# Causal convolution and top-2 mixture of experts: memory of their own for block rows, and the second and third unit's convolution shared anew

## The chip, the cores and the metric

One core of one Trainium2 chip. The metric is the device time of one execution in microseconds, before against after; the time before is the median of three runs. A profile is one further execution, seen by the hardware profiler.

Engines: TensorE (PE; PEld is its weight load), VectorE (DVE), ScalarE (ACT), GpSimd (POOL) and SyncE (SP), which here only issues DMAs. A name with a q behind it (SPq) is an engine's queue of issues.

## The reference

```python
def _attn_ref(x, weight):                    # x (8, 3584, 192), weight (8 heads, 7 taps)
    w = softmax(weight, axis=-1)
    x_pad = np.concatenate([np.zeros((B, 6, D)), x], axis=1)
    x_unf = x_pad[:, idx, :].reshape(B, S, K, H, group)       # 7 rows up to the token's own
    return np.einsum('hk,bskhg->bshg', w, x_unf).reshape(B, S, D)

def _moe_ref(x, w_gate, w_noise, noise, w1, w2):   # 28672 tokens, 8 experts, 192 -> 1024 -> 192
    noisy_logits = x @ w_gate + np.log1p(np.exp(x @ w_noise)) * noise
    top2 = ...                               # the two largest, softmax of the two: top2_w
    for e in range(E):
        for k in range(2):
            mask = top2[:, k] == e
            h = np.maximum(x[mask] @ w1[e], 0.0)
            out[mask] += top2_w[mask, k, None] * (h @ w2[e])
```

## The kernel before

The 28672 tokens are worked on in 28 units of 1024 tokens (128 partitions with 8 tokens each). A unit is convolved (`conv`, or on TensorE by `conv_pe` with a diagonal 128 x 128 matrix for each head and tap), scaled by a power of two and split into a high and a low float16 part (`rb`), gated (`gating`: transposes, 40 small matmuls, log1p, the top two, the rank in each expert's list), and then each token's row is scattered twice to a region in DRAM, `xs`, by 16 indirect DMAs of GpSimd. Rounds of blocks read these regions: in round j each expert takes one block (128 rows in round 0, 256 after). A block loads its rows transposed (`load_block`, tile `bT`), multiplies them with `w1` in two halves of 512 hidden columns (`mm1`, five float16 matmuls for each 128 columns), takes the Relu on ScalarE and its low part on VectorE (`h`), multiplies with `w2` (`mm2`), scales by the gate on ScalarE and adds to the output by an indirect DMA of GpSimd. `load_meta` loads the token numbers and gates of a round's rows, once for all experts. Blocks are loaded two ahead.

The weights are prepared in place, part by part (`prepare`): a part (e, c) is scaled on ScalarE into a float16 high part, and the low part is the difference, taken on VectorE or, for nine parts in `POOL_LO`, on GpSimd; then ScalarE writes the scaled original too. A part's high and low half lie where the part before it lay as loaded, so the next part's ScalarE step waits for the low part of the one before. Parts 0 and 1 of an expert are `w1`, 2 and 3 are `w2`. Gram products on TensorE give the scales, for two experts at a time; `allsum` is a small matmul that adds over partitions.

The order on TensorE, VectorE, ScalarE and SyncE is that of the program; GpSimd's is found by the scheduler. The program's order is written out by hand for the first three units, in `ORDER`. Each letter is one step of a generator in `streams`: `a`, `b`, `e`, `E` a head on TensorE for units 0, 1, 2, 2; `c`, `d`, `f` the rest of the convolution of units 0, 1, 2 (maximum, scale, split); `g`, `h`, `i` the gating of units 0, 1, 2; `w` a step of the preparation; `v`, `V` evacuations of unit 2's heads from PSUM; `1`, `2` the six rows that a unit takes over from the unit before (`halo`); `D` diagonals; `l`, `x` loads. The text up to the first bar runs before the blocks; each part between bars is the side work of one slot, and a block has two slots, one behind each half of `mm1`. When the parts are used up, `Side.slot` fills the slots by itself, by a credit in microseconds (`FREE`) against each step's planned cost, the number that it yields.

Memory: the diagonals are in a pool `start` that is closed when the written order is over; the pool `ffn` (`bT`, `mt`, `h`, `y`) is opened in the memory that becomes free. PSUM has two buffers `ph` and two `py`; unit 1 and the second half of unit 2 use `ph`, the first half of unit 2 `py`.

Of the kernel before, what the change touches and what calls it, by code (L numbers as in the profile page):

```python
# [19 lines left out]
P = 128  # L20
# [5 lines left out]

ORDER = "Daaaacwccc1xcnwcwcgnwglgggbbwbwggwgwbbwwwbbbww2eeeedddwdwddvhEEwhEEhhh|hw|hw|hww|ww|ww|Vfw|fw|fw|fww|fww|fww|iww|iww|ii|i|i|i|i"

# [4 lines left out]
def kernel(  # L33
# [44 lines left out]
    cpool = ctx.enter_context(tc.tile_pool(name="cpool", bufs=1))  # L78
    rpool = ctx.enter_context(tc.tile_pool(name="rpool", bufs=1))
    small = ctx.enter_context(tc.tile_pool(name="small", bufs=2))  # L80
    dram = ctx.enter_context(tc.tile_pool(name="dram", bufs=1, space=DRAM))
# [301 lines left out]
    def conv_pe(u, hs, tag="ph"):  # L383

        cps.setdefault(u, [])
        nh = 4 if tag == "ph" else 2
        for n, h in enumerate(hs):
            if n % nh == 0:
                cps[u].append((h, psum.tile([P, nh, BIG], F32, name=tag, bufs=2)))
            for k in range(K):  # L390
                nc.tensor.matmul(cps[u][-1][1][:, n % nh, :TU * G].rearrange("p (t g) -> p t g", g=G), diag[h, k],  # L391
                                 xts[u][:, k:k + TU, h * G:(h + 1) * G], start=(k == 0), stop=(k == K - 1))
            yield 3.0
# [11 lines left out]
    def conv(u, hs=range(H)):  # L405
# [28 lines left out]
        for h0, c in ps:  # L434
            for h in range(4):
                V.tensor_tensor(xc[:, :, (h0 + h) * G:(h0 + h + 1) * G],
                                c[:, h, :TU * G].rearrange("p (t g) -> p t g", g=G),
                                xsc[:, :, None].to_broadcast([P, TU, G]), op=OP.mult)
# [155 lines left out]
    def load_meta(j):  # L594
        start, T = rounds[j]
        mt = ffn.tile([P, E, 2, 8], F32, name="mt", padded_shape=[P, E, 2, 8])
        for h in range(T // P):
            ld = nc.sync.dma_start(
                mt[:, :, h, :],
                dview(xsf, (start + h * P) * ROWF + 192, [[ROWF, P], [REG * ROWF, E], [1, 8]]))  # L600
            loads(ld, j)
        return mt
# [85 lines left out]
    def load_block(j, e):  # L688
        start, T = rounds[j]
        xT = ffn.tile([P, 3, BIG], F16, name="bT", bufs=3)  # L690
        r0 = e * REG + start
# [4 lines left out]

    HH = H // 2
    diagonals(range(HH))
# [19 lines left out]
    def batch(g, n):  # L718
# [3 lines left out]
        yield from g  # L722

    streams = {
        "a": conv_pe(0, range(HH)), "c": batch(conv(0, range(HH, H)), K * (H - HH)), "n": gates, "g": gating(0),
        "b": conv_pe(1, range(H)), "d": conv(1, []), "h": gating(1), "e": conv_pe(2, range(HH), "py"), "E": conv_pe(2, range(HH, H)), "f": conv(2, []), "i": gating(2),
        "v": once(evacuate, 2, range(HH)), "V": once(evacuate, 2, range(HH, H)), "D": once(diagonals, range(HH, H)), "1": once(halo, 1), "2": once(halo, 2), "l": late_loads(), "x": once(load_x, 2),
        "w": prep,
# [19 lines left out]
    class Side:  # L748
# [45 lines left out]
        def slot(self, k, T, rate, spent=0.0):  # L794
            self.pace()
            if stages:
                steps(stages.pop(0))
                return
            self.age += BLOCK / 2 * T / BIG
            self.credit = min(self.credit, 0.0) + FREE[k] * T / BIG * rate - spent  # L800
            self.route(k)
            cut = False
# [85 lines left out]
    with tc.If(total > 0):  # L888
        ctr = small.tile([P, 1], F32, name="ctr")
        for e in range(E):  # L890
            nb = nc.values_load(noi[0:1, e:e + 1], engines=engines, min_val=0, max_val=N // P)
            V.memset(ctr, float(cap))
            with tc.For_i(0, nb, 1) as i:
                row = i * P + (e * REG + cap)
                xT = ffn.tile([P, 3, BIG], F16, name="bT", bufs=3)
                nc.sync.dma_start(xT[:, :, :P], xs[bass.ds(row, P), 0:384], transpose=True)
# [35 lines left out]
```

## Time and profile before

| | us |
|---|---|
| median of 3 runs | 2208.21 (2207.07 to 2211.52) |
| the profiled execution | 2218.51 |
| its span, first to last instruction | 2216.4 |
| TensorE busy in the span | 2070.0 (93%) |
| VectorE busy | 1519.5 (69%) |
| ScalarE busy | 795.4 (36%) |
| GpSimd busy | 1337.5 (60%) |
| TensorE's mean granted clock | 0.973 |

The times in the trace count from the span's start; 2.1 us of the profiled execution lie around the span. The granted clock is a share of 2.4 GHz; its lower level is 0.5, that is 1.2 GHz. A float32 matmul appears as two instructions.

### The profile page before, as it was taken

To read this page: it belongs to the slowest core of one execution; us is meant where nothing else is said; L and a number is where in the kernel's file an instruction comes from. 1 tells how busy PE (TensorE), PEld (TensorE's weight loads), DVE (VectorE), ACT (ScalarE), POOL (GpSimd) and SP (SyncE) were. 2 spreads that over 40 slices of the span, in tenths; PEclk is the share of its full clock that TensorE was granted. 3 is DMA by queue.
4 is the path that set the end of the run, shared out by engine and by line. 5 is a ranking of instruction groups with operands and counts; after the bars stand their busy time and mean duration, and the time that the engine had idled before them with its cause. 6 is when DMAs were issued, how large, how long until landed. Compare 5 with 4: busy or idle time off the path is not lost.

```text
span 2216.4 us, 53349 instructions
## 1 busy us (share of the span) xinstructions
PE 2070.0 (93%) x22182; PEld 1929.7 (87%) x22182; DVE 1519.5 (69%) x3975; ACT 795.4 (36%) x1169; POOL 1337.5 (60%) x923
## 2 busy tenths in 40 slices
PE   6768799999999989999999999999999999999997
PEld 5757788888898888899999898999999999999997
DVE  6467777888888877787778777687777874423332
ACT  5254333333333333333333333333333333333332
POOL 0353646766778767667766576557766676543333
PEclk9888999999999999999999999999999999999999
DMA  8523656566666566466655566466665666443332
GB/s 231 170 63 60 140 95 100 97 108 112 120 113 126 109 108 119 73 112 116 117 98 87 105 118 113 70 107 116 117 105 82 112 102 106 74 57 47 50 50 34
DMA packets 462773, 223.65 MB, mean 101 GB/s; under 512 B 342152, under 2 KB 449720, under 8 KB 462393
## 3 DMA queue, kind: packets, MB, share of 16 engines
q1 hardware_dynamic: 375352, 129.38, 29.1%
q0 software_dynamic: 87168, 90.76, 27.2%
q8 instruction: 175, 2.87, 0.5%
q14 instruction: 78, 0.64, 0.1%
HBM read 40.12 MB, written 115.38 MB: 70 GB/s over the span
## 4 chain that ended last, share of the span: by engine, by line
PE 67%; DVE 12%; DMA 4%; issue 4%; SPq 4%; another core or an unknown queue 3%; ACT 3%; POOL 2%; POOLq 0%; DVEq 0%; ACTq 0%
PE ph L658 33%; PE py L672 32%; DVE h L662 3%; SPq L475 3%; DVE xc L415 3%; ACT h L661 2%; POOL out_dram L676 1%; DMA xT<-rb 1%; DMA out_dram<-y,ids 1%; POOL xs L570 1%; PE misc L484 1%; PE ph L391 1%; DVE t L511 0%; DVE w1s L286 0%
## 5 line engine op out<-in xcount | busy, mean ns | idle before, releaser
L676 POOL DMA_INDIRECT out_dram<-y,ids x456 | 805.4, 1766 | 508.5 <-ACT y L675 309.6
L658 PE MATMUL ph<-bT,w1s 128*128 128x256 f16 (+1 forms) x9280 | 1054.4, 272 | 37.6 <-issue 8.5
L658 PEld LDWEIGHTS <-w1s 128*128 128x128 f16 x9280 | 892.8, 98 | 146.3 <-issue 29.2
L672 PE MATMUL py<-w2s,h 128*128 128x192 f16 x10944 | 971.0, 249 | 33.2 <-DVE h L662 23.6
L672 PEld LDWEIGHTS <-h 128*128 128x128 f16 x10944 | 922.3, 99 | 53.8 <-DVE h L662 30.7
L662 DVE SCALAR_TENSOR_TENSOR h<-ph,h 128x1024 f16<-128x1024 f32 (+1 forms) x464 | 557.6, 1202 | 568.4 <-ACT h L661 524.7
L661 ACT ACTIVATE h<-ph 128x1024 f16<-128x1024 f32 (+1 forms) x464 | 466.9, 1008 | 621.0 <-PE ph L658 494.0
L570 POOL DMA_INDIRECT xs<-rb,idx x448 | 513.9, 1147 | 270.9 <-issue 199.5
L415 DVE SCALAR_TENSOR_TENSOR xc<-xt,wt,xc 128x192 f32<-128x192 f32 x1224 | 418.7, 409 | 0.3 <-DMA xt<-zero 0.3
L675 ACT ACTIVATE y<-py,ga 128x192 f32<-128x192 f32 x456 | 190.0, 419 | 619.4 <-PE py L672 451.6
L391 PE MATMUL ph<-xt,dg 128*128 128x192 f32 x224 | 46.0, 375 | 14.0 <-DMA xt<-zero 12.9
L391 PEld LDWEIGHTS ph<-xt,dg 128*128 128x128 f32 x224 | 44.6, 226 | 14.2 <-ACT dg L381 12.8
L413 DVE TENSOR_SCALAR xc<-xt,wt 128x192 f32<-128x192 f32 x204 | 53.0, 323 | 4.4 <-DMA xt<-in_x_dram 4.4
L484 PEld LDWEIGHTS <-xT 128*128 128x128 f16 x1120 | 33.8, 96 | 24.5 <-DMA xT<-rb 23.0
L484 PE MATMUL misc<-ghi,xT 128*128 128x16 f16 x672 | 34.6, 170 | 21.6 <-DMA xT<-rb 20.8
L283 POOL TENSOR_TENSOR w1s<-w1s,w1s 128x1024 f16<-128x1024 f32 x5 | 10.7, 2144 | 69.7 <-ACT w1s L329 69.6
L426 DVE TENSOR_REDUCE am<-xc 128x8 f32<-128x1536 f32 (+1 forms) x27 | 46.4, 1718 | 0.4
L441 DVE TENSOR_TENSOR xc<-xc,xs 128x1536 f32<-128x1536 f32 (+1 forms) x27 | 46.5, 1722 | 0.0
L511 DVE SCALAR_TENSOR_TENSOR t<-t,t 128x64 f32<-128x64 f32 x168 | 40.1, 239 | 5.8
L503 ACT ACTIVATE t<-t 128x64 f32<-128x64 f32 x28 | 7.2, 256 | 98.3 <-DVE t L501 85.3
L446 ACT ACTIVATE rb<-xc 128x1024 f16<-128x1024 f32 x28 | 29.4, 1050 | 17.1 <-DMA xs<-rb,idx 7.2
L449 DVE TENSOR_TENSOR rb<-xc,rb 128x1024 f16<-128x1024 f32 x28 | 34.1, 1216 | 0.8 <-DMA out_dram<-y,ids 0.4
(143 smaller groups left out, 695.4 us busy)
## 6 DMA issues: line engine op xcount, KB each, us to landing
out_dram<-zero SPq DMA_DIRECT2D x28, 768.0 KB
xt<-in_x_dram SPq DMA_DIRECT2D x27, 768.0 KB
out_dram<-y,ids POOLq DMA_INDIRECT x456
xs<-rb,idx POOLq DMA_INDIRECT x448
w2s<-in_moe_w_dram SPq DMA_DIRECT2D x16, 384.0 KB
w1s<-in_moe_w_dram SPq DMA_DIRECT2D x8, 512.0 KB
w1s<-in_moe_w_dram SPq DMA_DIRECT2D x16, 256.0 KB
bT<-xs SPq DMA_TRANSPOSE x232
```

What stands on the lines that cost most here:

```text
L391: nc.tensor.matmul(cps[u][-1][1][:, n % nh, :TU * G].rearrange("p (t g) -> p t g", g=G), diag[h, k], xts[u][:, k:k + TU, h * G:(h + 1) * G ...
L413: V.tensor_scalar(dst, src, wt[:, h, k:k + 1], None, op0=OP.mult)
L415: V.scalar_tensor_tensor(dst, src, wt[:, h, k:k + 1], dst, op0=OP.mult, op1=OP.add)
L475: nc.sync.dma_start(xT[:, t], rb[:, t, 0:384], transpose=True)
L484: nc.tensor.matmul(lg[:, t], xT[:, t, c, :], g[:, gc], start=(i == 0), stop=(i == len(seq) - 1))
L570: s = nc.gpsimd.indirect_dma_start(out=xsf, out_offset=bass.IndirectOffsetOnAxis(ap=idx[:, k, t:t + 1], axis=0), in_=rbf[:, t, :], in_offs ...
L658: nc.tensor.matmul(ph[:, f, :T], w1_part(e, wc, lo, half * nf + f), xT[:, c, :T], start=(i == 0), stop=(i == len(seq) - 1))
L661: halves.append(nc.scalar.activation(hh[:, hs, :T], ph[:, :, :T], AF.Relu))
L662: V.scalar_tensor_tensor(hl[:, hs, :T], ph[:, :, :T], 0.0, hh[:, hs, :T], op0=OP.max, op1=OP.subtract)
L672: nc.tensor.matmul(py[:, :D], a[:, f, ts], w2_part(e, lo, f), start=(n == 0), stop=(n == 3 * FC - 1))
L675: nc.scalar.activation(y, py[:, :D], AF.Copy, scale=gate[:, h:h + 1])
L676: a = nc.gpsimd.indirect_dma_start(out=out, out_offset=bass.IndirectOffsetOnAxis(ap=ids[:, h:h + 1], axis=0), in_=y, in_offset=None, compu ...
```

## The change

`bT` and `mt` move to a pool `io`, opened before the diagonals' pool. Unit 1 is convolved on TensorE for six heads (eight before), for the last two on VectorE in one batch of 14 instructions. Unit 2 is convolved on TensorE for four heads (all eight before), for the other four on VectorE in four groups of seven instructions, spread over slots; `E` and `V` are gone, and 42 diagonals are made, not 56. `ORDER` is new: eight more steps of preparation stand before the blocks (24 in place of 16), and the written order goes on for 21 slots (18 before). In the last nine of these slots, preparation and the third unit's convolution are also taken up by credit.

```diff
-ORDER = "Daaaacwccc1xcnwcwcgnwglgggbbwbwggwgwbbwwwbbbww2eeeedddwdwddvhEEwhEEhhh|hw|hw|hww|ww|ww|Vfw|fw|fw|fww|fww|fww|iww|iww|ii|i|i|i|i"
+ORDER = "Daaaacwccc1xcnwcwcgnwglgggbbwbwggwwgbbwwwwbdwwwwdd2eeeedwwdwddvhwwhwwhhhw|hw|hw|hww|www|ww|ww|ww|ww|wwf|wf|ff|ff|ff|ff|i|i|ii|i|i|i|i"
...
+    io = ctx.enter_context(tc.tile_pool(name="io", bufs=2))
...
-                cps[u].append((h, psum.tile([P, nh, BIG], F32, name=tag, bufs=2)))
+                cps[u].append((h, psum.tile([P, nh, BIG], F32, name=tag, bufs=2)[:, :min(nh, len(hs) - n)]))
...
-            for h in range(4):
+            for h in range(c.shape[1]):
...
-        mt = ffn.tile([P, E, 2, 8], F32, name="mt", padded_shape=[P, E, 2, 8])
+        mt = io.tile([P, E, 2, 8], F32, name="mt", padded_shape=[P, E, 2, 8])
...
-        xT = ffn.tile([P, 3, BIG], F16, name="bT", bufs=3)
+        xT = io.tile([P, 3, BIG], F16, name="bT", bufs=3)
...
-    HH = H // 2
+    HH, HP = H // 2, H - 2
...
+    def group(g, k, n):
+        for _ in range(n // k):
+            for _ in range(k):
+                next(g)
+            yield
+        yield from g
+
...
-        "b": conv_pe(1, range(H)), "d": conv(1, []), "h": gating(1), "e": conv_pe(2, range(HH), "py"), "E": conv_pe(2, range(HH, H)), "f": conv(2, []), "i": gating(2),
-        "v": once(evacuate, 2, range(HH)), "V": once(evacuate, 2, range(HH, H)), "D": once(diagonals, range(HH, H)), "1": once(halo, 1), "2": once(halo, 2), "l": late_loads(), "x": once(load_x, 2),
+        "b": conv_pe(1, range(HP)), "d": batch(conv(1, range(HP, H)), K * (H - HP)), "h": gating(1), "e": conv_pe(2, range(HH), "py"), "f": group(conv(2, range(HH, H)), 7, K * (H - HH)), "i": gating(2),
+        "v": once(evacuate, 2, range(HH)),  "D": once(diagonals, range(HH, HP)), "1": once(halo, 1), "2": once(halo, 2), "l": late_loads(), "x": once(load_x, 2),
...
             self.pace()
-            if stages:
+            fixed = bool(stages)
+            if fixed:
                 steps(stages.pop(0))
-                return
+                if len(stages) > 8:
+                    return
             self.age += BLOCK / 2 * T / BIG
             self.credit = min(self.credit, 0.0) + FREE[k] * T / BIG * rate - spent
-            self.route(k)
+            if not fixed:
+                self.route(k)
```

## Rows read from the trace of the kernel before

**Rows 1.** The page's first part: busy time of each engine, its share of the span, and the number of instructions.

```profile
PE 2070.0 (93%) x22182; PEld 1929.7 (87%) x22182; DVE 1519.5 (69%) x3975; ACT 795.4 (36%) x1169; POOL 1337.5 (60%) x923
```

**Rows 2.** Stretches of the span, from the table by windows: the stretch, its length, then the busy time (and number of instructions) of PE, PEld, DVE, ACT and POOL, the granted clock, the DMA engines' share and GB/s.

```profile
54.00:89.00 35.00, 27.44 (x137) 25.48 (x134) 15.29 (x50) 8.13 (x9) 18.19 (x17) 0.82 0.93 272
...
121.70:190.50 68.80, 45.93 (x592) 42.82 (x592) 47.62 (x114) 39.20 (x52) 36.70 (x27) 0.88 0.31 62
...
264.60:279.00 14.40, 2.23 (x39) 1.56 (x39) 4.00 (x7) 1.68 (x2) 6.39 (x4) 0.61 0.99 172
279.00:285.00 6.00, 6.00 (x44) 5.68 (x45) 4.88 (x16) 0.68 (x2) 1.19 (x1) 0.51 0.35 64
...
340.00:354.50 14.50, 11.04 (x135) 9.09 (x133) 9.19 (x29) 2.74 (x5) 9.29 (x6) 0.95 0.43 77
354.50:2000.00 1645.50, 1593.55 (x17324) 1485.86 (x17323) 1221.90 (x3234) 586.10 (x853) 1102.44 (x756) 0.99 0.60 103
```

**Rows 3.** TensorE in order of time, 54 to 112 us: start, time, line, operation, out<-in, shape, number, and in brackets the idle time before it and what ended it. L391 is the convolution, L149 the sum over partitions, L466 the gating's transposes, L658 a block's first product.

```profile
54.09 14.32 PE L391 MATMUL ph<-xt,dg 128*128 128x192 f32 x70
68.25 0.28 PE L149 MATMUL misc<-tr,ones 128*128 128x4 f32 x2
...
91.09 2.53 PE L466 MATMUL ph<-ident,rb 128*128 128x128 f16 x22 [0.31 <-DVE rb L451]
94.74 7.66 PE L391 MATMUL ph<-xt,dg 128*128 128x192 f32 x28 [1.11 <-ACT xT L467]
103.24 4.80 PE L391 MATMUL ph<-xt,dg 128*128 128x192 f32 x28
111.56 0.72 PE L658 MATMUL ph<-bT,w1s 128*128 128x128 f16 x5 [3.53 <-DMA bT<-xs]
```

**Rows 4.** Waits of SyncE's queue and of VectorE in the first 110 us (who waited for whom, total us, times, the longest), and VectorE's instruction behind the longest one.

```profile
SPq L598 <- PE ph L391: 25.7, 1, 25.7
...
DVE wf L307 <- remote: 18.8, 1, 18.8
...
78.85 0.16 DVE L307 TENSOR_SCALAR wf<-misc 128x4 int32<-128x4 int32 x1 [18.79 <-remote]
```

**Rows 5.** TensorE's waits from 111.5 to 200 us.

```profile
PE ph L658 <- DVE w1s L286: 7.8, 4, 3.8
PE ph L658 <- DVE h L662: 6.8, 2, 5.6
PE misc L541 <- DVE M L536: 4.7, 1, 4.7
PE ph L658 <- ACT w1s L327: 4.2, 2, 3.3
...
PE ph L658 <- ACT xc L401: 2.2, 1, 2.2
```

**Rows 6.** SyncE's queue in order of time around 260 us: L598 loads a round's meta data, L159 zeroes rows, L475 transposes unit 3 for its gating.

```profile
254.08 1.00 SPq L598 DMA_DIRECT2D mt<-xs  x2
...
257.08 8.87 SPq L159 DMA_DIRECT2D xs<-zero  x8
266.06 11.25 SPq L475 DMA_TRANSPOSE xT<-rb  x8
```

**Rows 7.** The longest wait of SyncE's queue from 300 to 356 us.

```profile
SPq L598 <- DMA xs<-rb,idx: 12.9, 2, 12.2
```

**Rows 8.** GpSimd in order of time: the first and the last of unit 0's 16 scatters (L570), and the first subtraction behind them (L283, part (2,0)); then VectorE's instruction that ran beside it and the one ahead of it.

```profile
57.02 1.15 POOL L570 DMA_INDIRECT xs<-rb,idx  x1 [3.67 <-DVE gj L273]
...
76.69 0.96 POOL L570 DMA_INDIRECT xs<-rb,idx  x1 [0.30 <-issue]
83.70 2.12 POOL L283 TENSOR_TENSOR w1s<-w1s,w1s 128x1024 f16<-128x1024 f32 x1 [6.05 <-ACT w1s L329]
...
83.84 2.02 DVE L139 TENSOR_SCALAR xs<-xf 128x8 int32<-128x8 int32 x1
85.89 0.17 DVE L140 TENSOR_SCALAR xf<-xf 128x8 int32<-128x8 int32 x1
```

**Rows 9.** ScalarE in order of time: unit 2's halo (L373), the copies of unit 1's transposes (L467), and a weight part's step (L327).

```profile
61.05 1.15 ACT L373 ACTIVATE xt<-xt 128x1152 f32<-128x1152 f32 x1
...
92.81 2.79 ACT L467 ACTIVATE xT<-ph 128x2048 f16<-128x2048 f16 x2 [0.80 <-PE ph L466]
95.48 1.15 ACT L327 ACTIVATE w1s<-w1s,ws 128x1024 f16<-128x1024 f32 x1
```

**Rows 10.** The first and the last line of the 56 Gram products of experts 2 and 3 on TensorE.

```profile
46.81 1.18 PE L268 MATMUL grams<-w1s 128*128 128x128 bf16 x16
...
49.74 0.87 PE L268 MATMUL grams<-w2s 128*128 128x128 bf16 x12
```

**Rows 11.** The first and the last of unit 1's log1p on VectorE.

```profile
104.35 0.20 DVE L505 TENSOR_SCALAR t<-t 128x64 f32<-128x64 f32 x1 [0.32 <-ACT t L503]
...
108.26 0.23 DVE L515 TENSOR_TENSOR ns<-t,l 128x64 f32<-128x64 f32 x1
```

**Rows 12.** The convolution of four heads of unit 0 on VectorE, in order of time, and from the page the group of all low parts `h` (busy time, mean ns of one, idle time before them and what ended it).

```profile
11.57 1.01 DVE L413 TENSOR_SCALAR xc<-xt,wt 128x192 f32<-128x192 f32 x4 [4.39 <-DMA xt<-in_x_dram]
12.83 7.99 DVE L415 SCALAR_TENSOR_TENSOR xc<-xt,wt,xc 128x192 f32<-128x192 f32 x24 [0.26 <-DMA xt<-zero]
...
L662 DVE SCALAR_TENSOR_TENSOR h<-ph,h 128x1024 f16<-128x1024 f32 (+1 forms) x464 | 557.6, 1202 | 568.4 <-ACT h L661 524.7
```

More of the change, by code (lines that the diff above doesn't have):

```diff
@@ L894 @@
                 row = i * P + (e * REG + cap)
-                xT = ffn.tile([P, 3, BIG], F16, name="bT", bufs=3)
+                xT = io.tile([P, 3, BIG], F16, name="bT", bufs=3)
                 nc.sync.dma_start(xT[:, :, :P], xs[bass.ds(row, P), 0:384], transpose=True)
```

## The prediction, made before the changed kernel had run

> **What bounds the kernel now.** I read the page's busy line first: TensorE is busy for 93% of the span, VectorE 69%, GpSimd 60% [rows 1]. The table by stretches then says where the other 7% lies [rows 2]: from 354.5 to 2000 us TensorE loses only 3%, but four short stretches before it lose 7.6 + 22.9 + 12.2 + 3.5 = 46 us (length less TensorE's busy time). The change works in that part alone. What I did next was to name the wait that ends last in each stretch.
>
> From 54 to 111.56 us (first matmul of the first block) the two convolutions on TensorE set the time: 70 instructions for unit 1, 56 for half of unit 2 right behind them, and 56 for its other half, in 7.66 and 4.80 us [rows 3]. SyncE holds the first load of meta data for 25.7 us, until the last matmul that reads a diagonal [rows 4], because the `ffn` pool lies where the diagonals lie. VectorE stands still for 18.8 us [rows 4]: its scale waits for a small matmul queued behind the 70. That matmul is recorded as over at 68.53 [rows 3], VectorE goes on at 78.85 [rows 4]. These 10.3 us no row explains, and the profiled execution (2218.51) is 10.3 us longer than the median (2208.21). I can't say whether the timed runs have this wait; it is carried below as a term that is in or out.
>
> From 121.7 to 190.5 us (seven blocks of 128 rows) VectorE is busy 69%, ScalarE 57%, TensorE 67% [rows 2]: a chain, not an engine, is the limit. The waits name it: 7.8 + 4.2 us for weights being prepared, 6.8 us for `h`, 2.2 us for the evacuation `V` [rows 5]. The last two are one thing: the second half of unit 2 sits in one of two `ph` buffers until `V`. Then 14.4 us are lost from 264.6 [rows 2], where gating(3) waits for transposes: SyncE first waited for scatters, until 254.08, then zeroed rows, 8.9 us, and only then issued the transposes, 11.3 us [rows 6]. Last, 3.5 us are lost around 350 [rows 2], behind 12.2 us of SyncE waiting for scatters [rows 7].
>
> **Term A, up to block 1 (121.74 before).** Removed: 28 TensorE instructions of unit 1, 56 of unit 2 (7.66 + 4.80 us), 14 diagonals, the wait for the diagonals. But halo(2) now stands behind five more weight activations on ScalarE, and the last two of them must wait for GpSimd's subtraction of part (2,0). GpSimd isn't ordered by hand; the subtraction comes after the 16 scatters in the program, and these run from 57.02 to 77.65 [rows 8]. So: 77.65 + 2.12 (subtraction) = 79.8; two weight activations at 1.15 [rows 9], 82.1; halo, 1.15, 83.3. Only then can the 56 instructions of unit 2 begin, where before they began behind the small matmul of 68.25 [rows 3].
>
> TensorE will have idled some 19 us. After the 14.4 us at 264.6 the granted clock stood at 0.51 for 6 us [rows 2], and the 28 instructions at 94.74 took 0.27 us each against 0.17 [rows 3]. I take 6 us at 0.32 (19 instructions) and 37 at 0.165: 12.1 us, end 95.4. The Trainium skill ("TensorE: Matmul & The Clock Gate", Part 1) says that the throttled clock is the default and that activity lifts it; it speaks against this order of work as the row does, and a sum that ignored it would have 9.2 us here and A 3 us better.
>
> Then the Gram products of experts 4 and 5, 3.8 us [rows 10], now ahead of the first block, 99.2; transposes, 2.5 [rows 3], and the end of their copies, 2.0 [rows 9], 103.7; 40 gate matmuls, 1.0 (from 102.2 to 103.24, before the last of unit 2 [rows 3]); first block matmul at 105, 6.5 us earlier. Six weight activations now lie between those copies and the gating's Exp on ScalarE (6 us from the same rows): Exp at 110. Behind it on VectorE: 4.2 us of log1p [rows 11], 1.2 of meta data and 0.7 for `h` (a half block of the 1.2 us in [rows 12]), and 3.1 for the top two by the planner's figure in the code; 119.2. The rank matmuls wait for that and block 1 is queued behind them: 120.2 against 121.74. A = -1.5. Bounds: the subtraction between the scatters as soon as it is ready (about 71), -8; all 56 at the slow rate, +4.
>
> **Term B, blocks 1 to 7 (121.74 to 190.53).** The extra VectorE work: 28 convolution instructions of unit 2, 4 x 0.25 + 24 x 0.333 = 9.0 us [rows 12], and 1 for unit 3. Out: traces of experts 4 and 5 (2.6), gating(2)'s first steps (2.0, later now), one preparation (1.2), and some 3 us of collisions with GpSimd's subtractions, which move ahead of the blocks: a VectorE instruction took 2.02 us instead of 0.17 while one ran [rows 8]. So 47.6 becomes 48.8. TensorE's own path is 68.8 less the waits that lose their cause: 5.6 and 2.2 (`ph` has both buffers) and 12.0 (weights are a block or two ahead): 49. Two paths of 49 us that feed each other don't give 49; at 87% they give 56 or 57. B = -12. Bounds: VectorE at its present 69%, 0 or a little over; at 100%, -18.
>
> **Term C, blocks 8 to 12.** Unit 3's convolution begins five slots earlier, but gating(2) is three slots later, so both meet in blocks 8 to 10: convolution 53 x 0.333 and maximum 1.75, gating 0.6 + 4.1 + 3.1 + 2.8 by the planner's figures, `h` 6 x 1.2 [rows 12]: 37.3 us of VectorE for three blocks that TensorE does in 25.5. Against that stands the present 4.7 us wait for the rank in the same place [rows 5], and the block of slack. C = +4, from 0 to +9.
>
> **Term D, the 14.4 us.** By the planner's credits unit 3 is convolved by slot 25, two slots sooner, so its transposes are issued before the meta load of round 2, not behind it. They need 8.9 + 11.3 us of SyncE and about 3 to land; four slots, 17 us, pass until TensorE wants them. The stall is 7 us instead of 14.4: D = -7, from -14 to 0.
>
> **Term E.** With gating(3) earlier its scatters end earlier: -2.5, from -4 to 0. What moves on SyncE besides costs nothing: the meta data and the first two blocks are loaded from about 84 on and are there by 88, 17 us before TensorE wants them; without that cover the present 3.5 us wait [rows 3] would return. The 14 diagonals that ScalarE no longer makes lie in the first 24 us, where TensorE works on unit 0 in any case.
>
> **Sum.** -1.5 - 12 + 4 - 7 - 2.5 = -19 on the profiled execution: 2218.5 to 2199.5. If the unexplained 10.3 us are in the timed runs, these go from 2208.2 to 2189; if not, A is worse by them, and they go to 2199.5. Half of it: 2194.
>
> **The rivals.** *More is gained:* the subtraction slips between the scatters (A -8), VectorE runs near 100% (B -18), and no stall is left in D: -8 - 18 + 4 - 12 - 3 = -37, less half of 10.3: 2176. For it: the scatters leave 0.3 us gaps, and GpSimd's order is the scheduler's. Against: they are all ready first. *Nothing measurable:* the wait at 68.5 exists only in the profile (+10.3), and VectorE takes back what weights and buffers give (B -8, C +8): -1.5 + 10.3 - 8 + 8 - 7 - 2.5 = -0.7; 2207.5. VectorE's 42 added instructions speak for it. *Slower:* halo(2). Its place behind GpSimd starves TensorE for 19 us in the very stage that was meant to shrink. If the first block matmul comes later than about 112, where the timed run before may have had it at 101, A is +14 there; the weights prepared meanwhile then give only B -6, with C +7 and D -5: +10, 2218. It is decided by when the subtraction of part (2,0) runs: later than about 86 us, and this case holds. *The new pool does nothing:* SyncE loads unit 3's rows first, into the buffer that halo(2) still reads, so meta data can't come before 83 either way; as the blocks can't start by then, this costs no more than the 3.5 us wait for `bT` [rows 3], and lies inside the range.
>
> **How the numbers follow.** Forecast 0.45, more gained 0.17, nothing 0.2, slower 0.18. Within 0.2% (4.4 us) is about what a measurement can't tell from no change. The forecast's own range is 2186 to 2203, all of it faster; faster 0.62 with the second case, same 0.2, slower 0.18. The 8-in-10 range takes in the upper gain and the no-change case and cuts the slow one's upper half: 2176 to 2213.
>
> **What would show it.** Right: unit 2's halo at 83 us and TensorE idle before it; no wait of SyncE for a diagonal; block 1 at about 120, the first full Relu at 178 to 182; no wait for `w1s` above 1 us; the gate's stall near 270 halved; the rank's wait in blocks 8 to 10 grown. Wrong: block 1 before 114 or after 126; the stall at 264 as long as before; VectorE above 95% in blocks 4 to 10.

## The result: slower, where faster was forecast

The kernel after takes 2228.72 us (median of 4 runs, 2227.48 to 2231.83) against 2209.86 for the kernel before in the same set of runs (median of 4): 1.0087 of it, with a 95% interval from 1.0067 to 1.0106. That is 18.9 us slower. The forecast was 2194, in a range from 2176 to 2213. The profiled execution of after took 2227.48 (span 2225.0), that of before 2218.51, so the two profiles differ by 9.0 us only. Where the other 10 come from is the first question for the runs.

Line numbers of after are one higher than those of before. First its busy line and its table by stretches, which answer to [rows 1, 2].

```profile
PE 2051.9 (92%) x22098; PEld 1907.0 (86%) x22098; DVE 1527.6 (69%) x4018; ACT 790.2 (36%) x1154; POOL 1339.1 (60%) x923
```

```profile
54.00:89.00 35.00, 10.01 (x53) 9.71 (x53) 19.43 (x65) 12.86 (x15) 24.69 (x19) 0.67 0.90 256
...
121.70:190.50 68.80, 53.52 (x647) 48.40 (x646) 52.52 (x133) 31.86 (x45) 33.62 (x24) 0.88 0.36 75
...
264.60:279.00 14.40, 7.51 (x81) 6.66 (x82) 3.29 (x19) 0.57 (x2) 0.24 (x1) 0.55 0.46 81
...
354.50:2000.00 1645.50, 1590.94 (x17297) 1480.30 (x17295) 1217.22 (x3228) 582.80 (x848) 1100.59 (x754) 0.99 0.59 103
```

TensorE has 18 us less to do (84 convolution matmuls fewer) and the kernel is longer. From 54 to 89 us TensorE works 10.0 us, where it worked 27.4. Its order of time shows the hole (answers to [rows 3]):

```profile
58.34 2.52 PE L392 MATMUL ph<-xt,dg 128*128 128x192 f32 x14
85.85 11.37 PE L392 MATMUL py<-xt,dg 128*128 128x192 f32 x56 [24.99 <-ACT xt L374]
...
105.20 2.39 PE L659 MATMUL ph<-bT,w1s 128*128 128x128 f16 x40
120.77 0.21 PE L542 MATMUL misc<-M,before 128*128 128x64 f16 x1 [13.18 <-DVE M L537]
```

And GpSimd and ScalarE, in order of time, say why (answers to [rows 8, 9]): the last scatter, the subtraction of part (2,0), the activation that waited for it, unit 2's halo (L374), and unit 1's row copy (L447).

```profile
79.28 0.96 POOL L571 DMA_INDIRECT xs<-rb,idx  x1 [0.30 <-issue]
80.25 2.14 POOL L284 TENSOR_TENSOR w1s<-w1s,w1s 128x1024 f16<-128x1024 f32 x1
```

```profile
82.42 1.15 ACT L328 ACTIVATE w1s<-w1s,ws 128x1024 f16<-128x1024 f32 x1 [12.91 <-POOL w1s L284]
83.60 1.15 ACT L330 ACTIVATE w1s<-w1s,ws 128x1024 f32<-128x1024 f32 x1
84.65 1.15 ACT L374 ACTIVATE xt<-xt 128x1152 f32<-128x1152 f32 x1
...
87.50 1.04 ACT L447 ACTIVATE rb<-xc 128x1024 f16<-128x1024 f32 x1
```

This is the chain that the prediction named, to within 3 us at each link. What it stands against is another matter, below. In the stages behind, TensorE's waits from 121.7 to 300 us (answers to [rows 5]):

```profile
PE misc L485 <- DMA xT<-rb: 10.5, 6, 4.7
PE py L673 <- DVE h L663: 8.0, 6, 4.8
...
PE misc L542 <- DVE M L537: 4.3, 1, 4.3
PE py L467 <- DVE rb L450: 2.9, 1, 2.9
PE ph L659 <- DVE w1s L287: 2.5, 1, 2.5
```

The waits for weights went from 12.0 to 2.5 us, nearly as forecast (none above 1 us); the gate's wait for transposes by DMA (12.0 us before) and the waits for `h` did not go. Of the other signs that the prediction named, unit 2's halo, block 1 at about 120 and no wait of SyncE for a diagonal came true. The first full Relu came at 184.75, not at 178 to 182, and the rank's wait in blocks 8 to 10 did not grow (4.3 us after 4.7).

### The profile page after: what moved, and what is told of

Its sections match the earlier page's. It is cut to its first block, busy times and chain, and to the rows that moved or that the text cites. A ratio compares the mean times of both kernels' runs of the same rounds, so it can differ in the third digit from the quotient of the medians.

```text
span 2225.0 us, 53210 instructions
## 1 busy us (share of the span) xinstructions
PE 2051.9 (92%) x22098; PEld 1907.0 (86%) x22098; DVE 1527.6 (69%) x4018; ACT 790.2 (36%) x1154; POOL 1339.1 (60%) x923
## 4 chain that ended last, share of the span: by engine, by line
PE 69%; DVE 10%; SPq 3%; another core or an unknown queue 3%; ACT 3%; issue 3%; DMA 2%; POOL 1%; ACTq 0%; DVEq 0%; POOLq 0%
PE py L673 34%; PE ph L659 34%; DVE h L663 3%; SPq L476 3%; DVE xc L416 2%; ACT h L662 2%; DMA xT<-rb 1%; PE misc L485 1%; DVE xc L414 1%; ACT y L676 1%; DVE t L512 0%; DMA out_dram<-y,ids 0%; POOL xs L571 0%; DVE am L427 0%
## 5 line engine op out<-in xcount | busy, mean ns | idle before, releaser
L571 POOL DMA_INDIRECT xs<-rb,idx x448 | 518.6, 1158 | 269.8 <-issue 198.5
L416 DVE SCALAR_TENSOR_TENSOR xc<-xt,wt,xc 128x192 f32<-128x192 f32 x1260 | 430.5, 408 | 0.2 <-DMA xt<-zero 0.2
L485 PE MATMUL misc<-ghi,xT 128*128 128x16 f16 x672 | 36.0, 170 | 21.2 <-DMA xT<-rb 16.4
L427 DVE TENSOR_REDUCE am<-xc 128x8 f32<-128x1536 f32 (+2 forms) x28 | 46.9, 1674 | 0.3
L442 DVE TENSOR_TENSOR xc<-xc,xs 128x1536 f32<-128x1536 f32 (+2 forms) x28 | 47.0, 1678 | 0.0
L447 ACT ACTIVATE rb<-xc 128x1024 f16<-128x1024 f32 x28 | 29.4, 1049 | 33.2 <-DVE xc L442 13.4
L392 PE MATMUL ph<-xt,dg 128*128 128x192 f32 x140 | 26.4, 353 | 12.0 <-ACT dg L382 12.0
L485 PE MATMUL misc<-glo,xT 128*128 128x16 f16 x448 | 35.3, 170 | 1.2 <-issue 1.2
```

Of the source, the lines that this page charges most:

```text
L416: V.scalar_tensor_tensor(dst, src, wt[:, h, k:k + 1], dst, op0=OP.mult, op1=OP.add)
L442: V.tensor_tensor(v, v, xsc[:, :, None].to_broadcast([P, TU, len(hs) * G]), op=OP.mult)
L485: nc.tensor.matmul(lg[:, t], xT[:, t, c, :], g[:, gc], start=(i == 0), stop=(i == len(seq) - 1))
L571: s = nc.gpsimd.indirect_dma_start(out=xsf, out_offset=bass.IndirectOffsetOnAxis(ap=idx[:, k, t:t + 1], axis=0), in_=rbf[:, t, :], in_offs ...
```

## The experiments

They ran in four sets, each on a chip of its own, numbered 8, 4, 13 and 5 on record and called the later chips below. The number of the chip of the result above isn't on record, so it may be one of these; it is called the first chip. On the later chips before has medians of 2149.85, 2152.04, 2147.72 and 2149.25 us. Each ratio is to before in the same set of runs; ratios of different sets are compared here because these medians agree within 0.2%. Single executions of one kernel spread by 1% there (before: 2139.89 to 2165.3 in one set), so verdicts rest on the ratios and not on one profile. Before's profile from chip 8 took 2161.84 us, 12 us more than the median of its set, that of the front restored 7.5 us less than its own: behind block 28, differences of some 10 us between two profiles decide nothing. The profiles tell where the time lies; this table has, from each kernel's trace, the start of blocks 0 and 1 (first `ph<-bT` matmul) and how long three stretches of blocks took, in us:

| kernel | chip | ratio to before, 95% interval | block 0 | block 1 | 1 to 8 | 8 to 28 | 28 to 231 |
|---|---|---|---|---|---|---|---|
| before | first | 1 | 111.6 | 121.7 | 66.3 | 206.7 | 1797.2 |
| after | first | 1.0087 [1.0067, 1.0106] | 105.2 | 121.1 | 61.3 | 211.6 | 1804.8 |
| before | 8 | 1 | 94.4 | 103.4 | 62.5 | 207.3 | 1762.4 |
| after | 4 | 1.0168 [1.0134, 1.0201] | 107.9 | 123.8 | 61.6 | 204.3 | 1773.8 |
| halo(2) early | 8 | 1.0121 [1.0083, 1.016] | 95.6 | 111.3 | 61.9 | 205.0 | 1768.6 |
| front restored | 4 | 1.0082 [1.0057, 1.0106] | 89.9 | 100.2 | 66.9 | 204.6 | 1761.6 |
| front restored, three row buffers | 13 | 0.9972 [0.9954, 0.999] | 90.9 | 100.6 | 68.2 | 205.1 | 1734.2 |
| after, three row buffers | 5 | 1.0052 [1.0035, 1.0069] | 106.0 | 121.9 | 61.2 | 202.9 | 1743.0 |
| before, three row buffers | 5 | 0.9939 [0.9907, 0.997] | 92.8 | 100.5 | 63.4 | 200.2 | 1738.9 |

**Before again.** No edit.

> The kernel before, profiled a second time. Two readings of the 10.3 us in which VectorE stood still after the small matmul of 68.53 us. Reading one, the wait belongs to that one execution and not to the timed runs: then it is absent here, VectorE's power of two of unit 1 starts at about 69 us instead of 78.85, the first block matmul at about 101 us instead of 111.56, block 1 at about 111, and the span is about 2206. Then the whole 10.3 us, and not half of it, had to be added to the front of the kernel after. Reading two, the wait is in the program: then the first block starts at 111.6 us again and the span is about 2216.

Reading one. In order of time, TensorE's first part, and VectorE's instruction that had waited 18.8 us:

```profile
55.27 11.62 PE L391 MATMUL ph<-xt,dg 128*128 128x192 f32 x70
66.73 0.28 PE L149 MATMUL misc<-tr,ones 128*128 128x4 f32 x2
66.87 9.35 PE L391 MATMUL py<-xt,dg 128*128 128x192 f32 x56
...
80.56 4.82 PE L391 MATMUL ph<-xt,dg 128*128 128x192 f32 x28 [1.52 <-ACT xT L467]
...
94.41 1.53 PE L658 MATMUL ph<-bT,w1s 128*128 128x128 f16 x20 [3.39 <-DMA bT<-xs]
```

```profile
67.05 0.16 DVE L307 TENSOR_SCALAR wf<-misc 128x4 int32<-128x4 int32 x1 [5.73 <-PE misc L149]
```

VectorE goes on 0.04 us after the small matmul, not 10.3. The wait is 5.72 or 5.73 us in this and in the five other profiles with before's front (below); so 18.79 belongs to one execution.

Beside this profile, the first one's block 0 is 17.2 us later and its block 1 18.3, not 10.3. Not all of that is the wait. The 70 convolution matmuls, which ran ahead of it, took 14.32 instead of 11.62 us; the granted clock was 0.53 from 54 to 60 us there and 1.00 here, and the small matmul was over 1.5 us later. Behind the wait, the transposes and the third group of 28 matmuls (7.66 instead of 4.82 [rows 3]) took some 5 us more, at granted clocks of 0.71 and 0.65 where this profile has 1.00. So one execution had a slow front, in which the wait is the largest part.

It is also more than the 10 us that were asked for: without those 18.3 us the first chip's two profiles would differ by 27 us, and its medians differ by 18.9. Whether its timed runs were free of all of it stays open. (The front of after starts its blocks within 3 us of each other on the first chip and on chip 4, so the front can be set beside the first chip's.) The expected span of 2206 carried the first chip's time over and says nothing here.

**halo(2) early.**

```
-...bbwwwwbdwwwwdd2eeeed...
+...bbwwwwbd2wwwwddeeeed...
```

> The kernel after, with the halo of unit 2 issued on ScalarE ahead of the five weight activations instead of behind them; nothing else moves. Theory one (the front: halo(2) behind GpSimd's subtraction starves TensorE): the 56 convolution matmuls of unit 2 start at about 62 us instead of 85.9, TensorE's busy time from 54 to 89 us rises from 10 to about 20 us, and the first block starts at about 98 instead of 105.2, because then unit 1's rows, whose copy on ScalarE (87.6 us) stands behind the same weight activations, are next to come late. Time 2229 less 7: about 2222. Theory two (the loss is VectorE's, in the blocks 8 to 12): the first block may come earlier, but by block 13 the gain is gone; time 2227 to 2229.

1.0121 against after's 1.0168 (the latter from the next set of runs, on chip 4): some 10 us back. TensorE has its 56 matmuls at 61.68, and stops one link further on. Its waits from 40 to 123 us:

```profile
PE ph L467 <- ACT rb L447: 12.8, 1, 12.8
PE misc L542 <- DVE M L537: 12.6, 2, 11.7
```

Unit 1's row copy on ScalarE stood behind the same weight activations, so unit 1's gating begins late. The rank matmul's wait of 11.7 us is no third delay: from the first gate matmul to the rank matmul, behind which block 1 is queued, it is 17.1 us here (93.89 to 110.95) and 16.6 in before's undisturbed profile (85.21 to 101.79). The gating's Exp, behind six weight activations, holds VectorE for 1.9 us only. The halo was the first of two victims, not the cause; the cause is weight activations that wait for GpSimd, queued ahead of the chain of unit 1.

**After again.** No edit; the control for all that follows.

> The kernel after, unchanged, beside the next three. Both theories: first block at 105 to 108 us, block 1 at 121 to 124, block 28 some 18 to 22 us after the undisturbed profile of before, and a time 19 to 30 us above before's.

Block 0 and 1 as on the first chip, within 3 us. Block 28 is 16.5 us behind that of before's undisturbed profile, a little less than expected, but the time is 37 us above before's, more than the 19 to 30 expected. The ratio, 1.0168, is twice the first chip's.

**Front restored.** The hand order ahead of the blocks has halo(2), the row copies and the weights nearly in before's order; the rest of after stays. Seven steps of preparation move behind the first bar, three from ahead of halo(2) and four from behind it.

```
-bbwwwwbdwwwwdd2eeeedwwdwddvhwwhwwhhhw|hw|hw|hww|www|ww|ww|ww|ww|
+bbwwwwbdw2eeeedddwdwddvhwhwhhh|hww|hww|hwww|www|www|www|www|www|
```

> The kernel after, with the hand order ahead of the first block put back to that of before as far as halo(2) and the weights go (four steps of the preparation fewer ahead of halo(2), seven of the twelve steps behind it handed to the block stages); memory pools and the shared convolution stay those of after. Theory one (the whole loss is the front: halo(2), unit 1's row copies and gating(1)'s Exp on ScalarE stand behind weight activations that wait for GpSimd): first block at 92 to 96 us, block 1 at 101 to 105 where before has it at 103.3 undisturbed, and a time 15 to 19 us below that of the kernel after, so that of before within 5 us. Theory two (the loss is in the block stages: VectorE's added instructions and unit 3's early convolution): the front gains, but blocks 1 to 28 take 12 to 18 us longer than the 270 us of before, and the time stays 15 us or more above before's.

Block 1 starts at 100.2, 23.6 us earlier than in after; blocks 1 to 8 give 5.3 of it back, since the weights are prepared there again. Timed: 1.0082, half of the loss. The front is shown as that half; theory one's "within 5 us of before" fell. Theory two's blocks 1 to 28 fell as well: they took 271.5 us, before's 269.8. So the other half does not lie there.

**Unit 3 on TensorE, in the front restored and in before.**

```
-NRB, NPE = 2, 3
+NRB, NPE = 2, 4
```

> The kernel of the front restored, and unit 3's rows transposed on TensorE as those of units 0 to 2 are, no longer by SyncE's DMA (one constant). It is to tell what bounds blocks 8 to 28, which took 204 to 212 us in every profile so far, whatever was moved in them. If it is the transposes of unit 3 by DMA (12 to 15 us of TensorE waiting), those waits go, TensorE gets some 3 us of transposes more, blocks 8 to 28 take 192 to 197 us, and the time is 8 to 12 us below that of the front restored. If it is VectorE's chain of unit 3 and 4, the wait moves to the next unit's gate or to the rank, and the time moves by under 4 us.

> The kernel before, with unit 3's rows transposed on TensorE. If the DMA transposes of unit 3 bound blocks 8 to 28, 8 to 12 us below before. If another chain does, within 4 us of before.

1.0062 [1.004, 1.0083], hardly below the front restored, and 1.0049 [1.0022, 1.0075]: slower than before, which neither reading had expected. Blocks 8 to 28 still take 204.0 and 200.4. TensorE's waits from 285 to 480 us of the second kernel:

```profile
PE misc L484 <- DMA xT<-rb: 19.0, 7, 14.1
PE py L672 <- ACT y L675: 11.5, 1, 11.5
```

The wait for transposes has moved to unit 4, whole (14.1), and behind it stands a second one of 11.5. (In the same profile ScalarE's row copy waits 17.1 us for scatters: the wait that *Before, early credit* finds below.) Taking away the stall of [rows 2, 6] shortened neither kernel.

**No early credit; no second-unit taps.** The slot rule of before in after, and after with unit 2's convolution mostly left out:

```
-            if fixed:
-                steps(stages.pop(0))
-                if len(stages) > 8:
-                    return
+            if stages:
+                steps(stages.pop(0))
+                return
...
```

```
-                else:
+                elif u != 2:
                     V.scalar_tensor_tensor(dst, src, wt[:, h, k:k + 1], dst, op0=OP.mult, op1=OP.add)
```

> The kernel after, with the slot rule of before: while fixed stages are left, a slot runs its stage and returns, so that unit 3's convolution does not begin in the last eight of them. Theory two (unit 3's 53 convolution instructions meet gating(2) on VectorE and hold h up): the waits for the rank and for h from 200 to 230 us go, block 13 starts some 5 us earlier relative to block 8, but unit 3's transposes are issued later and the gate's stall near 270 us grows from 7.5 back towards 14; in all 2224 to 2229. Theory one: blocks 8 to 13 gain under 2 us, time 2228 to 2233.

> The kernel after, with 24 of the 28 convolution instructions of unit 2 on VectorE left out (the last tap alone stays, so unit 2's second half is not the reference's convolution). It takes 24 x 0.333 = 8.0 us of VectorE out of blocks 8 to 11. Theory two: VectorE is the limit there, so 5 to 8 us come back by block 13 and the time is about 2222. Theory one: VectorE's added work is hidden there, block 13 moves by under 2 us, time 2227 to 2229.

Without the early credit: 1.0207 [1.0179, 1.0236], not faster than after. Blocks 8 to 13 took 42.2 us instead of 55.3, as theory two had it, and 13 to 28 took 163.1 instead of 149.0: the gain is gone by block 28. (TensorE waits 18.1 us for blocks' rows, `bT<-xs`, from 200 to 480 us, where it was 2.7.) Without the taps: 1.0150 [1.0124, 1.0176], some 4 us below after, and the profile has the gain in blocks 1 to 8 (54.9 us against 61.6), not where theory two had put it: blocks 8 to 13 took 55.3 us with the taps and 55.2 without. The written order has these taps in slots 9 to 11, that is in blocks 4 and 5.

**No added taps at all**, in the front restored (`elif u not in (1, 2):`).

> The kernel of the front restored, with 36 of the 42 convolution instructions that the change gave VectorE left out (units 1 and 2 have there only the last tap of those heads, so part of their convolution is not the reference's). It takes about 13 us out of VectorE, 5 ahead of block 1 and 8 in blocks 8 to 11. If what is left of the loss is VectorE's added work: 10 to 15 us come back, 2153 to 2158. If it hides: 2164 to 2168, with at most 4 us in blocks 4 to 8.

1.0065 [1.0039, 1.0091] against 1.0082: 4 us, with intervals that overlap; blocks 1 to 8 took 61.4 instead of 66.9. VectorE's added instructions are at most a part of what is left of the loss.

**Before, weights earlier.**

```
-|hw|hw|hww|ww|ww|Vfw|fw|fw|fww|fww|fww|iww|iww|ii|i|i|i|i
+|hww|hww|hwww|www|www|Vfwww|fwww|fwww|fww|fww|f|i|i|ii|i|i|i|i
```

> The kernel before, with the steps of the weights' preparation in its block stages set as early as in the front restored (7 of 21 steps brought forward, 5 added); nothing else of the change. If the waits for weights in blocks 1 to 7 (w1s: 8.8 and 1.9 us) were on the path, they go to under 3 us and block 8 starts 6 to 9 us earlier after block 1; and if that lasts, the time is 5 to 8 us below before's. If what they hide is the gating's chain of VectorE and ScalarE, the rank's wait or h takes their place and the time is within 4 us of before's, or above it.

1.0037 [1.0016, 1.0058], and blocks 1 to 8 took 68.7 us, not fewer than 62.5. The waits of TensorE from 100 to 200 us:

```profile
PE misc L149 <- DVE pos L559: 7.5, 1, 7.5
PE ph L658 <- DVE h L662: 6.3, 3, 3.7
PE misc L541 <- DVE M L536: 4.2, 1, 4.2
PE ph L658 <- DVE w1s L286: 2.9, 1, 2.9
```

The wait for weights fell from 8.8 to 2.9 us, and a new one of 7.5 stands where TensorE's sum for the next weights' scale is queued, earlier now, behind VectorE's gating.

**Before, early credit.** After's slot rule in before.

> The kernel before, with the slot rule of after alone: in the last eight fixed stages the slot's credit is spent too, so that unit 3's convolution begins earlier. The kernel after without this rule was 1.0207 of before, with it 1.0168, so theory one has it as a gain: 4 to 8 us below before, the gate's stall for unit 3's transposes halved. The rival: it makes the side work of units 3 to 5 meet gating(2), the rank's wait in blocks 8 to 13 and the row copies' wait on ScalarE appear as in after, and the time is 4 us or more above before's.

1.0066 [1.004, 1.0092]: the rival. This rule alone makes before slower. Both waits that the rival named are in its profile: the rank's, 7.2 us where it was 4.7 (blocks 8 to 13 took 53.5 us instead of 47.5, but 8 to 28 not more than before's), and the row copies', 17.0 us on ScalarE and 11.5 on TensorE behind it. How the second comes about, the profile of after on chip 4 shows best. ScalarE, then TensorE, then GpSimd, in order of time around 400 us:

```profile
400.29 2.12 ACT L662 ACTIVATE h<-ph 128x1024 f16<-128x1024 f32 x2
420.65 1.06 ACT L447 ACTIVATE rb<-xc 128x1024 f16<-128x1024 f32 x1 [18.25 <-DMA xs<-rb,idx]
421.62 0.61 ACT L448 ACTIVATE rb<-xc 128x512 f16<-128x512 f32 x1
422.14 0.71 ACT L676 ACTIVATE y<-py,ga 128x192 f32<-128x192 f32 x2
```

```profile
405.43 4.53 PE L659 MATMUL ph<-bT,w1s 128*128 128x256 f16 x40
422.59 1.76 PE L673 MATMUL py<-w2s,h 128*128 128x192 f16 x10 [12.63 <-ACT y L676]
```

```profile
416.38 0.99 POOL L571 DMA_INDIRECT xs<-rb,idx  x1 [0.30 <-DMA out_dram<-y,ids]
417.67 0.99 POOL L571 DMA_INDIRECT xs<-rb,idx  x1 [0.30 <-issue]
422.81 1.61 POOL L677 DMA_INDIRECT out_dram<-y,ids  x1 [4.16 <-ACT y L676]
```

There are two row buffers. ScalarE copies a unit's rows into the buffer of the unit two before it, whose 16 scatters GpSimd issues a few at a time between the blocks' additions; the code lets the copy be issued once they are issued, not once they have landed. A convolution that begins sooner comes to that copy before the scatters are through. ScalarE then stands 18.25 us, the two evacuations `y` queued behind the copy free no `py` buffer, and TensorE stands 12.6. In the first chip's profile of after it was 10.8 us of ScalarE and 4.9 of TensorE at 409 to 421 us. The waits of ScalarE for `rb`, from 285 to 2050 us, of after on chip 4 and then of before on chip 8 (before's line is L446):

```profile
ACT rb L447 <- DMA xs<-rb,idx: 28.4, 3, 18.2
...
ACT rb L447 <- issue: 11.8, 2, 8.2
```

```profile
ACT rb L446 <- issue: 7.9, 1, 7.9
ACT rb L446 <- DMA xs<-rb,idx: 6.7, 1, 6.7
ACT rb L446 <- DVE t L509: 2.9, 1, 2.9
```

So before has the wait as well, at about half the length. In [rows 2]'s profile, on the first chip, before's row copies wait 7.2 us for scatters and after's 10.8; how much of the three per cent of TensorE's time lost there behind 354.5 us is due to it isn't shown.

**Three row buffers.** In the front restored and in after (with the meta data's pool undone to make room), in before (the third allocated once the diagonals are gone), and in before with the early credit.

```
-NRB, NPE = 2, 3
+NRB, NPE = 3, 3
-        mt = io.tile([P, E, 2, 8], F32, name="mt", padded_shape=[P, E, 2, 8])
+        mt = ffn.tile([P, E, 2, 8], F32, name="mt", padded_shape=[P, E, 2, 8])
```

```
-    NRB, NPE = 2, 3
+    NRB, NPE = 3, 3
...
-    for i in range(NRB):
+    for i in range(2):
...
+    rpool2 = ctx.enter_context(tc.tile_pool(name="rpool2", bufs=1))
+    rb = rpool2.tile([P, TU, ROW], F16, name="rb2")
+    V.memset(rb[:, :, 384:ROW], 0.0)
+    rbs.append(rb)
```

> The kernel of the front restored, with three row buffers (rb) instead of two, and the meta data's buffers back in the ffn pool to make room for the third. In the kernel after and in the front restored, ScalarE's copy of a unit's rows (L447) holds ScalarE's queue for 14 to 19 us near 383 to 420 us, waiting for the scatters that still read the row buffer, and TensorE stands for 8 to 13 us behind an evacuation y queued after it; before's trace has no such wait there. If that wait, which comes from convolving unit 3 five slots sooner, is most of what the front restored still lacks to before (15.6 us): the gap near 392 us goes, block 46 starts some 8 us earlier, and the time is 2157 to 2160. If the time is set by the side work as a whole and every gap closed opens another: block 46 gains, but the time stays at 2164 or above.

> The kernel before with a third row buffer (allocated once the diagonals' memory is free, so that it fits), nothing else. In the undisturbed profile of before ScalarE's queue stands in the row copies' wait for scatters 8.6 + 3.3 + 7.1 = 19 us, and TensorE has holes of 5.2 and 3.2 us behind it; in the kernel after it is 48 us, with holes of 12.6, 4.1 and 5.6. If the wait is before's own as well, a third buffer makes before 8 to 16 us faster, the kernel after is then to be charged only with the difference, and the front restored with three buffers (0.9972) has no gain left from the change. If the wait came only with the change: before moves by under 4 us.

> The kernel after with a third row buffer (meta data's buffers back in the ffn pool to make room), the front as it is in after. If front and row buffers are two losses that add: 1.0168 less the 0.0110 that the third buffer gave with the front restored, so 1.006, block 1 at 121 to 124 us as in after. If the row wait is only where the lost time of the front shows: below 1.002 or above 1.012.

> The kernel before with the slot rule of after and a third row buffer. With two buffers the rule cost 1.0066. If it cost that through the row copies' wait (17.4 us of ScalarE's queue at 381 us, a hole of 11.5 us on TensorE at 390 us): both are gone and it comes to that of before with three buffers or 3 to 8 us below it. If the rule costs through VectorE in blocks 8 to 13, it stays 8 us or more above before with three buffers.

The four pairs, as ratios to before:

| | two row buffers | three |
|---|---|---|
| before | 1 | 0.9939 [0.9907, 0.997] |
| before, early credit | 1.0066 [1.004, 1.0092] | 0.9942 [0.9922, 0.9962] |
| front restored | 1.0082 [1.0057, 1.0106] | 0.9972 [0.9954, 0.999] |
| after | 1.0168 [1.0134, 1.0201] | 1.0052 [1.0035, 1.0069] |

The third buffer is worth 0.61% to before and 1.1 to 1.24% wherever the early credit is on. The early credit costs before 0.66% with two buffers and, within intervals of 0.2 to 0.3% to either side, nothing with three, where blocks 8 to 13 still take 53.1 us: its loss went through the row copies' wait. Front and buffers add (1.0168 less 0.0110 would be 1.0058; measured 1.0052). By the profiles the gain lies from block 28 on: 1734 to 1743 us against 1762 to 1774 (for before this is more than the timed 13 us; its profile with two buffers is the long one named above). ScalarE's waits of the front restored with three, from 285 to 2050 us, have no row wait left:

```profile
ACT y L676 <- DMA out_dram<-y,ids: 65.4, 30, 4.8
...
ACT rb L447 <- DVE xc L442: 1.1, 1, 1.1
```

Three of these kernels beat both kernels of the case; the best, before with a third row buffer, has nothing of the change in it.

**Front restored, three row buffers, late credit.** Before's slot rule in that kernel.

> The front restored with three row buffers, and the slot rule of before. Tells whether unit 3's early convolution gains once it meets no row wait. If so, this is 4 to 10 us above the same kernel with the rule of after (0.9972), with the gate's wait for unit 3's transposes or a hole of TensorE from 300 to 400 us back; if the rule loses in blocks 8 to 13 (it cost 13 us there), this is 4 us or more below.

1.002 [1.0002, 1.0039], 10 us above the same kernel with the rule of after, and two waits of TensorE, of 10.8 and 6.2 us, end at 328 and 415 us. So in that kernel the rule earns its place; in after with two buffers it may (1.0207 without it, 1.0168 with it, with intervals that overlap); in before it earns nothing. Before convolves unit 2's second half on TensorE and these kernels late on VectorE; that this makes the difference wasn't tried.

## Why the prediction was wrong, step by step

**The sum,** on the two profiles of the first chip, by the starts of blocks: -19 us were forecast, +8.6 measured (the two spans).

| | forecast | measured |
|---|---|---|
| up to block 1 (A) | -1.5 | -0.6 |
| blocks 1 to 8 (B) | -12 | -5.1 |
| blocks 8 to 28 (C, D, E) | -5.5 | +4.9 |
| from block 28 on | 0 | +9.4 |

**Term A, the links: right.** Halo forecast to end at 83.3, it ended at 85.8; first block 105, measured 105.20; block 1 at 120.2, measured 121.1. The slow matmuls were there too: behind 25 us without a matmul the granted clock was 0.50 from 85.8 to 89.0 and 10 convolution matmuls took 3.15 us; from 92 to 97 it was 1.00 and 33 took 5.0. The Trainium skill ("TensorE: Matmul & The Clock Gate", Part 1) has the throttled clock as the default that activity lifts, which agrees. The slow matmuls cost 2.0 us on the 56 (11.37 against 9.37 with halo(2) early, where the pause before them was 0.94 us), not the 2.9 of the sum.

**Term A, what it was set against: this step failed.** The first block at 111.56 and block 1 at 121.74 were taken from an execution with a stall that was not seen again, and the stall was carried as 10.3 us, "in or out", at half. In before's profile on chip 8 block 1 is at 103.4 without it. Set against that, A is +17.7, and +20.4 with after's profile on chip 4, not -1.5 plus 5. The prediction's own rival *slower* had the mechanism, and put its point of decision at a subtraction "later than about 86 us", reckoned from a first block at 101; with the first block at 94.4 it held at 80.25 already. It had 0.18.

**Term B: mis-sized.** -12 forecast. Blocks 1 to 8 went from 66.3 to 61.3 us on the first chip, from 62.5 to 61.6 on the later ones: -5 and -1. Weights prepared ahead of the blocks are worth 5.3 us here (66.9 in the front restored, 61.6 in after), and the added convolution, which the sum let vanish into VectorE's idle time, costs 5.5 to 6.7: the one takes the other back. Weights only moved forward within the blocks' slots gained nothing; in before with the weights earlier, the wait moved to VectorE's gating. "At 87%, 56 or 57 us" was a guess at how two chains share; between the same two points after took 63.6 us (121.1 to the first full Relu at 184.75), so two paths of 49 us came to 77%.

**Terms C, D and E: not borne out.** +4, -7 and -2.5 were forecast, -5.5 over blocks 8 to 28 (E's stall, at 340 to 354.5 us, lies ahead of block 28, which starts at 394.8 in before). +4.9 was measured on the first chip. The -3.0 on the later chips confirms nothing: 200 to 207 us in every kernel there, whatever was moved. Blocks 8 to 13 took 7.6 us longer on the first chip (from 47.5 to 55.1). The transposes were issued ahead of round 2's meta load, as D had it, but the gate's wait for them fell from 12.0 to 10.5 only. (The 14.4 us that the prediction calls lost there are the length of the stretch; lost were 12.2, as in its own sum of 46.) What sets the 200 to 207 us was not found.

**All that lies behind 354.5 us was put at nothing: this step failed too.** "TensorE loses only 3%" there is 52 us, more than the 46 of the four stretches together, and the sentence that "the change works in that part alone" closed the door on it. From block 28 on after takes 7.6 us longer up to block 231 on the first chip and 11.4 on the later ones, in single profiles; that the change loses there is shown by the third row buffer, whose gain lies there and which gives after twice what it gives before. The early credit was read for what it would start sooner, not for what its next step waits for: the buffer that the unit two before it still holds. Taken out of after, it gave nothing back (1.0207): what it starts sooner pays there for the wait, while in before the wait is what is left of it.

**The account,** on the later chips, of 1.68%: front 0.80 to 0.86% (with three and with two buffers), the longer row wait 0.49 to 0.55% (what a third buffer gives the front restored, or after, more than before), 0.33% left, the distance of the front restored from before with three buffers each, of which VectorE's added taps may be half (0.17%, not resolved). By the intervals of the ratios in them, each of these differences is good to 0.3 to 0.5% only: the front is clear, the row wait just so, the rest is not clear of nothing. On the first chip the 18.9 us can't be divided so: its front shows the same times, its row wait was shorter, and no second profile of before was taken there.

The new pool gave and cost nothing that showed. No wait for a diagonal is left in after. With the meta data's half of the pool undone, in after with three buffers, SyncE's wait for the diagonals is back:

```profile
SPq L599 <- PE py L392: 10.8, 1, 10.8
```

It left block 1 where it was (121.9). The blocks' half of the pool, `bT`, was not tried alone.

## What to carry to other kernels

When one execution shows a stall that no row explains, profile the kernel again before forecasting from it; here the front of that execution was late by 18 us where the unexplained part was 10.3. A share that looks small ("only 3%") is to be turned into microseconds before it is set aside. When a step is issued earlier on an in-order engine, ask for each of its instructions what it waits for and who stands behind it on that engine, at the place where the new order first puts it and again some units later, when the buffers come round. If a stretch takes the same time whatever is moved in it, stop moving things in it and look at what lies behind: blocks 8 to 28 took 200 to 205 us with a third row buffer too, and the gain of that buffer, the largest of all, lay behind them.

## What the runs showed of the hardware that was not expected

- The same program took 2209.86 us in the first set of runs and 2147.72 to 2152.04 in the four later ones, on four chips, 2.6 to 2.8% less. The spans of before's two profiles differ by 56.5 us. TensorE is busy for 26.6 us less in the later one (2070.0 and 2043.4), and 21.2 us are waits of TensorE that end with nothing recorded (`issue`); after has 26.3 us of these on the first chip, and none of the sixteen later profiles has any. Where they come from isn't in the traces.
- One execution had VectorE wait 18.79 us for a matmul where six others had 5.72 or 5.73, with the matmul recorded as over 10.3 us before VectorE went on. In the same 10.3 us TensorE's next convolution matmuls have gaps of 4.3 us that end with nothing recorded. What held them isn't in the trace, and it was not seen again, so it could not be tried.
- A change's price differed by a factor of two between two sets of runs (1.0087 and 1.0168), with the same times in the front. A ratio of a few tenths of a per cent is to be taken as that of its own set.
